# A ResNet block with Winograd rows: side taps read in unbroken runs, and a last unit with its outer positions last

## The chip, the cores and the metric

One core of one Trainium2 chip runs the whole kernel. The metric is device time in microseconds, from the median of three runs; the profile is one further execution, whose span is counted from its first to its last instruction.

## What is computed

Input x is 2 x 512 x 64 x 64 in bf16. The block normalises groups of 128 channels, applies silu, convolves 3 x 3 (512 to 512 channels), adds an embedding of the time step, normalises, applies silu, convolves again, and adds x:

```python
h = conv3(_silu(gn(x, g1, be1)), w1)
emb = _silu(t_emb) @ w_emb
h = h + emb.reshape(B, C, 1, 1)
h = conv3(_silu(gn(h, g2, be2)), w2)
return x + h
```

## The kernel before, in words

**Tiles.** Each image (2 of them) is cut into two halves of rows, each layer so into four chunks, eight in all (numbers c = 0 to 7; 4 to 7 are the second convolution). A chunk has four units, one for each block k of 128 output channels; 32 units (u = 0 to 31). A plane is eight rows of 65 elements a partition: 32 even columns, one column of zeros, 32 odd columns (`RW` = 65).

**The transform.** Along the image's height the convolution runs as Winograd with six positions s: 0 to 3 are the inner ones, 4 and 5 the outer ones. The outer ones, and in the first chunks some of the inner, stay direct along the width: `plain_mms` sums three taps kx, each a matmul of 512 columns (eight rows x 64), over four blocks ct of input channels, so twelve matmuls into one bank of PSUM. Tap 1 is the centre; taps 0 and 2, the side taps, need the even columns' neighbours among the odd ones and the other way round. The remaining inner positions are nested along the width too: `B_mms` and `A_mms` each do two matmuls of 256 columns a block. B reads and writes 256 columns in one run; A reads one run and writes eight runs of 32 with gaps of 32.

**A unit of the second layer.** In the order of its code: position 4, B of positions 0 and 2, position 5, B of 1 and 3, A of 0 and 2, A of 1 and 3. ACT evicts each pair of banks (`evac_b`, `evac_pair`, `evac_o`), DVE combines: the S additions out of the evicted B (`s_ops`), their addition to the evicted A, then s, d, three scalings (8, 2 and 4; in the last chunk ACT does the one by 2), two writes of 16 rows into `ys` (y), and the outer positions' addition (O). The last line stores `ys` onto the output with an accumulating DMA from POOL's queue; x itself has been copied to the output earlier, DRAM to DRAM, by two transfers of SP's queue a unit. The intermediate buffers exist once: `MB` (four slots of 512, M(0) to M(3)), `SD`, `BT`.

**The order.** All operations are first recorded with a cost and the regions that they read and write; a planner (`Plan.solve`) lays them out as a list schedule by the longest way to the end, and the program is emitted in that order. Matmuls keep the order in which they were recorded. For each chunk the planes of the next one are produced beside its units: load, silu on ACT, row combinations on DVE (`rows_a`, `rows_b`).

**Lines.** Most operations are recorded by helpers, so the profile names the helper's line: L380 all matmuls, L329 two-operand operations of DVE, L333 scalings of DVE, L352 everything of ACT, L365 all DMAs, L369 memsets. The tile `ar` is the one arena in SBUF in which all buffers lie.

Of the kernel before, what the change touches and what calls it, by code (L numbers as in the profile page):

```python
# [184 lines left out]
RW = 65  # L185
# [29 lines left out]
def kernel(  # L215
# [460 lines left out]
    def plain_mms(bank, c, k, ct, s):  # L676
        md = mode(c)
        vo = vplane(c, ct, s)
        lst = []
        for i, kx in enumerate((0, 2, 1)):  # L680
            if s < 4:
                w = um0(k, ct, kx, s)
            elif md != "1":
                w = ur0(k, ct, s - 4, kx)
            else:
                w = A(st_off(ucnt[0] % 2, ct) + (s - 4) * 384 + kx * 128, [[1, 128]], BF16)
            off, st = ((32, -32), (0, 33), (33, -32))[kx]
            rhs = A(vo + off, [[RW, 8], [st, 2], [1, 32]])
            lst.append((Ps(bank, 0, [[1, 512]]), w, rhs, ct == 0 and i == 0, ct == CT - 1 and i == 2))
        return lst  # L690

    def B_mms(bank, c, k, ct, s):
# [18 lines left out]
    def unit(c, k, opening=0):  # L711
        l, b, ch = chunks[c]
        md = mode(c)
        u = ucnt[0]
        nm = f"u{c}{k}"
        if opening != 1:
            ufirst[u] = len(pl.ops)
        last = u == 31
        ys = YS[u % 2]
        M = lambda i, n=1, st=512: A(MB + i * 512, [[st, n], [1, 512]]) if n > 1 else A(MB + i * 512, [[1, 512]])  # L720
        if md == "1":
            BT, SD = BT1, SD1
            OO = [UREG[2 * (u % 2) + 1] + 9728, UREG[2 * (u % 2)] + 9728]
        else:
            BT, SD = BT0, SD0
            OO = [O0[u % 3] + PL, O0[u % 3]]
        if l == 0 and ch == 0 and b not in SSUM:
            SSUM[b] = (Fc(48), Fc(2 * CT))
        acc = lambda i: None
        if l == 0:  # L730
            cs, cq = SSUM[b]
            acc = lambda i: F(cs + 12 * k + 6 * ch + i)
        fid = ACT.Identity if l == 0 else ACT.Copy

        def evac_o(s, bank):
            act(A(OO[s - 4], [[RW, 8], [33, 2], [1, 32]]), Ps(bank, 0, [[1, 512]]), fid,
                scale=(0.25, 1.0)[s - 4], acc=acc(s), name=nm + f"o{s}")

        def evac_m(s, bank, i):
            act(M(s), Ps(bank, 0, [[1, 512]]), fid, scale=KAP[s], acc=i, name=nm + f"m{s}")  # L740

        def evac_pair(s, bank):
            act(M(s, 2, 1024), Ps(bank, 0, [[512, 2], [1, 512]]), ACT.Copy, scale=KAP[s], name=nm + f"m{s}")

        def evac_b(s, bank):
            if md == "0":
                act(A(BT, [[1, 256]]), Ps(bank, 0, [[1, 256]]), ACT.Identity, scale=0.5 * KAP[0], acc=acc(0), name=nm + "b")
                act(A(BT + 256, [[1, 768]]), Ps(bank, 256, [[1, 768]]), ACT.Copy, scale=0.5 * KAP[0], name=nm + "b")
            else:
                act(A(BT + s * 512, [[1024, 2], [1, 512]]), Ps(bank, 0, [[512, 2], [1, 512]]), ACT.Copy,  # L750
                    scale=0.5 * KAP[s], name=nm + "b")

        def run(steps, major=False):
            todo = [(st, ct) for st in steps for ct in range(CT)]
            if major:
                todo = [(st, ct) for ct in range(CT) for st in steps]
            for (bank, s, fn), ct in todo:
                mm(fn(bank, c, k, ct, s), nm + f"{fn.__name__[0]}{s}")

        nf = {"N": 0, "0": 2, "1": 4}[md]  # L760

        def s_ops():
            g = lambda q: A(BT + q * 256, [[512, nf], [32, 8], [1, 32]])
            o, st = (SD + 512, -512) if md == "0" else (SD, 512)
            tt(A(o, [[st, nf], [64, 8], [1, 32]]), g(0), g(1), AD, nm + "S")
            tt(A(o + 32, [[st, nf], [64, 8], [1, 32]]), g(0), g(1), SB_, nm + "S")

        if opening == 1:
            return [lambda: evac_o(4, 2 * k), lambda: evac_o(5, 2 * k + 1)]
        if md == "N":  # L770
            p1, p2 = (0, 2) if u == 0 else (next_pair(), next_pair())
            if not opening:
                run([(6, 4, plain_mms)])
                evac_o(4, 6)
            if u == 0:
                run([(p1, 2, plain_mms), (p1 + 1, 0, plain_mms), (p2, 1, plain_mms), (p2 + 1, 3, plain_mms)], True)
            else:
                run([(p1, 2, plain_mms), (p1 + 1, 0, plain_mms)])
            evac_m(2, p1, acc(1))
            evac_m(0, p1 + 1, None)  # L780
            if not opening:
                run([(7, 5, plain_mms)])
                evac_o(5, 7)
            if u:
                run([(p2, 1, plain_mms), (p2 + 1, 3, plain_mms)])
            evac_m(1, p2, acc(3))
            evac_m(3, p2 + 1, acc(2))
        elif md == "0":
            p1, p2, p3 = next_pair(), next_pair(), next_pair()
            run([(6, 4, plain_mms)])  # L790
            evac_o(4, 6)
            run([(p1, 2, B_mms), (p1 + 1, 0, B_mms)])
            evac_b(0, p1)
            s_ops()
            run([(7, 5, plain_mms)])
            evac_o(5, 7)
            run([(p2, 2, A_mms), (p2 + 1, 0, A_mms)])
            evac_m(2, p2, acc(1))
            evac_m(0, p2 + 1, None)
            tt(M(0, 2, 1024), M(0, 2, 1024), A(SD, [[512, 2], [1, 512]]), AD, nm + "A")  # L800
            run([(p3, 1, plain_mms), (p3 + 1, 3, plain_mms)])
            evac_m(1, p3, acc(3))
            evac_m(3, p3 + 1, acc(2))
        else:
            p1, p2, p3, p4 = next_pair(), next_pair(), next_pair(), next_pair()
            run([(6, 4, plain_mms)])
            evac_o(4, 6)
            run([(p1, 0, B_mms), (p1 + 1, 2, B_mms)])
            evac_b(0, p1)
            run([(7, 5, plain_mms)])  # L810
            evac_o(5, 7)
            run([(p2, 1, B_mms), (p2 + 1, 3, B_mms)])
            evac_b(1, p2)
            s_ops()
            run([(p3, 0, A_mms), (p3 + 1, 2, A_mms)])
            evac_pair(0, p3)
            run([(p4, 1, A_mms), (p4 + 1, 3, A_mms)])
            evac_pair(1, p4)
            tt(M(0, 4), M(0, 4), A(SD, [[512, 4], [1, 512]]), AD, nm + "A")

        tw = lambda off, st: A(off, [[st, 2], [1, 512]])
        tt(tw(SD, 512), M(0, 2), M(2, 2), AD, nm + "s")
        tt(M(0, 2), M(2, 2), M(0, 2), SB_, nm + "d")
        se = CFG["s"][c]
        scal(se[0], M(2), M(1), 8.0, nm + "8")
        scal(se[1], M(3), M(1), 2.0, nm + "2")
        scal(se[2], A(SD + 1024, [[1, 512]]), A(SD + 512, [[1, 512]]), 4.0, nm + "4")
        yr = lambda r0: A(ys + r0 * RW, [[RW, 16], [33, 2], [1, 32]])
        tt(yr(0), A(MB, [[0, 2], [1, 512]]), A(MB + 1024, [[512, 2], [1, 512]]), AD, nm + "y")
        tt(yr(16), A(SD, [[0, 2], [1, 512]]), A(SD + 1024, [[-512, 2], [1, 512]]), AD, nm + "y")  # L830

        yo = A(ys, [[24 * RW, 2], [1, PL]])
        oo = A(OO[1], [[OO[0] - OO[1], 2], [1, PL]])
        if CFG["oacc"][l] and not last:
            dma(yo.ap, oo.ap, [oo, yo], [yo], P * 4 * PL, nm + "oa", sw=True, acc=True)
        else:
            tt(yo, yo, oo, AD, nm + "O")
        yv = A(ys, [[1, YF]])
        if l == 0:
            dma(h_scr[b, k, ch], yv.ap, [yv], [K("h", b, k, ch)], P * YF * 2, nm + "st")  # L840
            act(A8(JNK, YF), yv, ACT.Square, scale=float(HW) ** -0.5, acc=F(cq + ch * CT + k), name=nm + "sq")
            if ch == 1 and k == CT - 1:
                later.append(lambda: gn2(b))
        else:
            dma(out[b, k, ch], yv.ap, [yv], [K("o", b, k, ch, i) for i in range(2)], P * YF * 2, nm + "out", sw=True, acc=True)
        ucnt[0] += 1

    later = []
# [193 lines left out]
    for c in range(8):  # L1042
        l, b, ch = chunks[c]
        for k in range(CT):
# [16 lines left out]
                    memz("gpsimd", A(UREG[j] + 9728 + 32, [[RW, 8], [1, 1]]), "oz")  # L1061
            if l == 1:
                stream_w2(ucnt[0] % 2, k)
                for i in range(2):
                    r0, r1 = i * YF // 2, (i + 1) * YF // 2
                    dma(out[b, k, ch][:, r0:r1], x[b, k, ch][:, RW + r0:RW + r1], [], [K("o", b, k, ch, i)],
                        P * YF * 1.4, f"pre{c}{k}", after=ufirst[max(ucnt[0] - CFG["pre"], 0)])
# [83 lines left out]
```

## Time and profile before

| | |
|---|---|
| median of three runs | 500.62 us (500.51 to 501.32) |
| profiled execution, its span | 500.2 us; 0.4 us below the median of the runs |
| PE busy | 465.6 us (93%) |
| DVE busy | 434.1 us (87%) |
| ACT busy | 382.5 us (76%) |
| POOL busy | 37.8 us (8%) |
| matmuls of 512 columns, f16 | 1248, 295.5 us |
| matmuls of 256 columns, f16 | 1408, 164.8 us |

Matmuls are pipelined: a duration in the profile holds the way through the array too, so two durations overlap, and differences between durations say more than the durations. A row of a timeline gives the start, the length, the engine, the line and the operation, and in brackets the idle time ahead of it with what ended it. The clock column is the share of TensorE's clock that was granted; it is 1.00 in all stages from 136 us on, and 0.86 on average between 74.5 and 136. The profile's chain that ended last consists to 22% of time that nothing explains and stops at DMA issues of POOL, so I read the stages instead.

### The profile page before, as it was taken

How to read it: one execution, taken by the hardware profiler on the slowest of the kernel's cores; microseconds unless marked ns; L12 is line 12 of the kernel's file. 1: busy time of each engine (PE TensorE's matmuls, PEld its weight loads, DVE VectorE, ACT ScalarE, POOL GpSimd, SP SyncE). 2: the span in 40 equal slices, each digit the busy share in tenths (PEclk: the TensorE clock that was granted, in tenths of full speed). 3: DMA queues.
4: the chain of work that ended last, by engine and by line, in shares of the span. 5: the costliest groups of instructions: out<-in, count | busy, mean ns of one | idle time of the engine just before them, and what ended most of it. 6: DMA issues, size and time to landing. Idle time of an engine off the chain costs nothing. (4 is left out here: it accounts for less than half of the span.)

```text
span 500.2 us, 8097 instructions
## 1 busy us (share of the span) xinstructions
PE 465.6 (93%) x2853; PEld 276.9 (55%) x2853; DVE 434.1 (87%) x856; ACT 382.5 (76%) x614; POOL 37.8 (8%) x66
## 2 busy tenths in 40 slices
PE   6999999686699999999999999999999999999980
PEld 5744344253345455555554567666666666666660
DVE  1699999997769999997999999997999999985553
ACT  4886899999699978679987887777765888565440
POOL 3100000000100000110000001103011110011000
PEclk9999999988599999999999999999999999999996
DMA  8754463465723336576576887677676768557232
GB/s 330 281 171 113 156 177 111 167 201 164 237 85 120 119 108 180 171 213 237 201 244 219 294 285 206 167 192 135 194 194 187 201 171 247 108 106 150 44 43 43
DMA packets 41064, 87.17 MB, mean 174 GB/s; under 512 B 6464, under 2 KB 16448, under 8 KB 41024
## 3 DMA queue, kind: packets, MB, share of 16 engines
q1 hardware_dynamic: 35808, 77.07, 46.5%
q0 software_dynamic: 4928, 9.59, 12.9%
q8 instruction: 22, 0.36, 0.3%
q14 instruction: 18, 0.15, 0.1%
q10 hardware_dynamic: 288, 0.01, 0.0%
HBM read 62.25 MB, written 31.85 MB: 188 GB/s over the span
## 5 line engine op out<-in xcount | busy, mean ns | idle before, releaser
L380 PE MATMUL psum<-ar 128*128 128x256 f16 (+2 forms) x2737 | 450.4, 326 | 9.0 <-DVE ar L329 4.3
L329 DVE TENSOR_TENSOR ar<-ar 128x1040 f16<-128x1040 f16 (+6 forms) x682 | 404.9, 651 | 39.5 <-ACT ar L352 35.1
L380 PEld LDWEIGHTS <-ar 128*128 128x128 f16 (+1 forms) x2729 | 264.3, 98 | 192.2 <-issue 16.1
L352 ACT ACTIVATE ar<-ar 128x384 bf16<-128x384 bf16 (+6 forms) x206 | 169.6, 854 | 45.6 <-DVE ar L329 41.6
L352 ACT ACTIVATE ar<-psum 128x512 f16<-128x512 f32 (+2 forms) x221 | 153.8, 718 | 51.1 <-PE psum L380 42.3
L352 ACT ACTIVATE ar<-ar,fs 128x2112 f16<-128x2112 bf16 (+1 forms) x32 | 68.6, 2148 | 6.9 <-DMA ar<-h_scr 5.1
L365 POOL DMA_DIRECT2D out_dram<-ar x16 | 19.3, 1207 | 129.1 <-DVE ar L329 129.0
L333 DVE TENSOR_SCALAR ar<-ar 128x512 f16<-128x512 f16 (+2 forms) x72 | 26.0, 382 | 2.0 <-ACT ar L352 2.0
L352 ACT ACTIVATION_READ_ACCUMULATOR ar<-psum 128x1 f32 x96 | 19.6, 204 | 0.0
L451 POOL TENSOR_TENSOR fs<-fs 128x1 f32<-128x1 f32 (+1 forms) x7 | 7.0, 996 | 138.2 <-DVE fs L449 138.2
L380 PE MATMUL psum<-ar,ones_bf 128*128 128x260 bf16 x64 | 9.5, 307 | 4.7 <-DMA ar<-in_x_dram 4.7
L369 POOL MEMSET ar<- 128x65 f16 (+4 forms) x27 | 4.1, 195 | 114.5 <-DVE ar L329 41.9
L380 PE MATMUL psum<-fs,ones_neg 128*128 128x1 f32 (+3 forms) x36 | 5.2, 258 | 7.0 <-DVE fs L982 6.9
L352 ACT ACTIVATION_READ_ACCUMULATOR ar<-ar 128x1 f32 x56 | 11.0, 197 | 0.0
L380 PEld LDWEIGHTS <-ones_bf 128*128 128x128 bf16 x64 | 6.6, 108 | 6.4 <-issue 3.4
L380 PEld LDWEIGHTS psum<-fs,ones_neg 128*128 128x128 f32 x36 | 5.0, 206 | 8.0 <-DVE fs L982 7.2
L365 POOL DMA_DIRECT2D ar<-ar x4 | 3.7, 930 | 72.3 <-DVE ar L329 56.4
L913 DVE SCALAR_TENSOR_TENSOR ar<-psum,ident 128x128 bf16<-128x128 f32 x4 | 1.2, 290 | 5.6 <-PE psum L380 5.6
L993 DVE BATCH_NORM_STATS2 fs<-ar 128x6 f32<-128x512 bf16 x8 | 5.3, 681 | 0.0
L442 DVE COPY fs<-psum 128x2 f32<-128x2 f32 (+1 forms) x7 | 1.1, 161 | 4.5 <-PE psum L380 4.5
L415 DVE CAST fs<-gparm 128x16 f32<-128x16 bf16 x1 | 0.2, 190 | 2.8 <-DMA gparm<-in_params_dram 2.8
L411 ACT ACT_TABLE_LOAD x1 | 1.3, 1283 | 1.7 <-PEq L1135 1.7
(49 smaller groups left out, 23.4 us busy)
## 6 DMA issues: line engine op xcount, KB each, us to landing
ar<-in_w_dram SPq DMA_DIRECT2D x32, 384.0 KB, 3.9
ar<-in_x_dram SPq DMA_DIRECT2D x16, 552.5 KB, 4.0
h_scr<-ar SPq DMA_DIRECT2D x16, 520.0 KB, 3.2
ar<-h_scr SPq DMA_DIRECT2D x16, 520.0 KB, 4.0
out_dram<-in_x_dram SPq DMA_DIRECT2D x32, 260.0 KB, 4.2
out_dram<-ar POOLq DMA_DIRECT2D x16, 520.0 KB, 6.4
u_scr<-ar SPq DMA_DIRECT2D x16, 384.0 KB, 3.2
ar<-u_scr SPq DMA_DIRECT2D x4, 1536.0 KB, 7.6
```

What stands on the lines that cost most here:

```text
L329: pl.op("DVE", 0.075 + 0.000521 * out.n, lambda: nc.vector.tensor_tensor(out=out.ap, in0=a.ap, in1=b.ap, op=op), regs(a, b), regs(out), name)
L333: pl.op("DVE", cost or 0.075 + 0.00026 * out.n, lambda: nc.vector.tensor_scalar(out=out.ap, in0=a.ap, scalar1=s, scalar2=None, op0=ALU.mul ...
L352: lambda: nc.scalar.activation(out=out.ap, in_=a.ap, func=func, scale=sc, **kw), regs(*rr), regs(*ww), name)
L365: lambda: eng.dma_start(out=out, in_=in_, **kw), regs(*r), regs(*w), name, lat=3.2 if sw else None, after=after, sw=sw)
L369: pl.op("POOL" if eng == "gpsimd" else "DVE", 0.08 + 0.0005 * out.n, lambda: e.memset(out.ap, v), (), regs(out), name)
L380: nc.tensor.matmul(out.ap, lhsT=lhsT.ap, rhs=rhs.ap, start=st, stop=sp, skip_group_check=True)
L411: nc.scalar.activation(out=fs[:, WARM:WARM + 1], in_=fs[:, WARM + 1:WARM + 2], func=ACT.Silu)
L415: nc.vector.tensor_copy(out=fs[:, GB:GB + 4 * CT], in_=gparm[:])
L442: pl.op("DVE", 0.16, lambda: V.tensor_copy(out=F(tot, 2 * n).ap, in_=ps.ap), regs(ps), regs(F(tot, 2 * n)), name)
L451: pl.op("POOL", 0.85, lambda: nc.gpsimd.tensor_tensor(out=F(rs, n).ap, in0=N.ap, in1=F(NEGH, n).ap, op=ALU.pow), regs(N), regs(F(rs, n)), ...
L913: pl.op("DVE", 0.3, lambda: nc.vector.scalar_tensor_tensor(out=j2.ap, in0=g.ap, scalar=1.0 / HW, in1=ident[:], op0=ALU.mult, op1=ALU.mult, ...
L993: pl.op("DVE", 0.61, lambda e=e, q=q: nc.vector.bn_stats(out=q.ap, in_=e.ap), regs(e), regs(q), nm)
```

## The change

Two places, and what follows from the second.

In `plain_mms` the side taps' read and write change places: the read takes 64 elements of a row as they lie, beginning at the row's first column (tap 0) or its second (tap 2), and the write puts the first 32 of each row to the odd and the second 32 to the even columns. The centre tap stays.

The last unit (u = 31) gets a function of its own. Its matmuls run in the order B, B, A, A, position 4, position 5. x is loaded into SBUF and not copied to the output beforehand; DVE adds it to d and s before the scalings, and writes y in pieces of eight rows in bf16. The output goes out in three plain stores from SP's queue: rows 8 to 23, then 24 to 31, then 0 to 7. Position 5 is not evicted by ACT; DVE adds it straight out of PSUM.

```diff
-            off, st = ((32, -32), (0, 33), (33, -32))[kx]
-            rhs = A(vo + off, [[RW, 8], [st, 2], [1, 32]])
-            lst.append((Ps(bank, 0, [[1, 512]]), w, rhs, ct == 0 and i == 0, ct == CT - 1 and i == 2))
+            if kx == 1:
+                rhs, o = A(vo, [[RW, 8], [33, 2], [1, 32]]), Ps(bank, 0, [[1, 512]])
+            else:
+                rhs, o = A(vo + kx // 2, [[RW, 8], [1, 64]]), Ps(bank, 32, [[64, 8], [-32, 2], [1, 32]])
+            lst.append((o, w, rhs, ct == 0 and i == 0, ct == CT - 1 and i == 2))
...
+        if last:
+            return last_unit(c, k, run, evac_b, evac_pair, evac_o, s_ops, M, SD, OO)
...
+    def last_unit(c, k, run, evac_b, evac_pair, evac_o, s_ops, M, SD, OO):
+        l, b, ch = chunks[c]
+        nm = "ul"
+        ys, yb, dx = YS[1], VB[0], VB[0] + 2112
+        xt = AB[acnt[0] % 2]
+        d = A(xt, [[1, YF]], BF16)
+        dma(d.ap, x[b, k, ch][:, RW:RW + YF], [], [d], P * YF * 2, nm + "x")
+        memz("gpsimd", A(yb + 32, [[RW, 32], [1, 1]], BF16), nm)
+        p1, p2, p3, p4 = next_pair(), next_pair(), next_pair(), next_pair()
+        run([(p1, 0, B_mms), (p1 + 1, 2, B_mms)])
+        evac_b(0, p1)
+        run([(p2, 1, B_mms), (p2 + 1, 3, B_mms)])
+        evac_b(1, p2)
+        s_ops()
+        run([(p3, 0, A_mms), (p3 + 1, 2, A_mms)])
+        evac_pair(0, p3)
+        run([(p4, 1, A_mms), (p4 + 1, 3, A_mms)])
+        evac_pair(1, p4)
+        run([(6, 4, plain_mms)])
+        evac_o(4, 6)
+        run([(7, 5, plain_mms)])
...
+        tt(M(0, 2, 1024), M(0, 2, 1024), tw(SD, 1024), AD, nm + "A")
+        tt(one(SD), M(0), M(2), AD, nm + "s")
+        tt(one(SD + 1024), M(2), M(0), SB_, nm + "d")
+        tt(tw(dx, 512), A(SD + 1024, [[0, 2], [1, 512]]), xr(0), AD, nm + "x")
+        tt(tw(dx + 1024, 512), A(SD, [[0, 2], [1, 512]]), xr(16), AD, nm + "x")
+        tt(M(1, 2, 1024), M(1, 2, 1024), tw(SD + 512, 1024), AD, nm + "A")
+        tt(M(0), M(3), M(1), SB_, nm + "d")
+        tt(M(2), M(1), M(3), AD, nm + "s")
+        ts(M(1), M(0), 2.0, nm + "2")
+        tt(row(yb, 8, BF16), one(dx + 512), M(1), AD, nm + "y")
+        ts(M(3), M(2), 4.0, nm + "4")
+        tt(row(yb, 16, BF16), one(dx + 1024), M(3), AD, nm + "y")
...
+        st(8, 16)
+        tt(row(ys, 24), one(dx + 1536), M(2), AD, nm + "y")
+        ts(M(1), M(0), 8.0, nm + "8")
+        tt(row(ys, 0), one(dx), M(1), AD, nm + "y")
+        tt(row(yb, 24, BF16), row(ys, 24), row(OO[0], 0), AD, nm + "O")
+        st(24, 8)
+        o5 = Ps(7, 0, [[1, 512]])
+        pl.op("DVE", 0.68, lambda: nc.vector.tensor_tensor(
+            out=row(yb, 0, BF16).ap, in0=row(ys, 0).ap, in1=o5.ap, op=AD), regs(row(ys, 0), o5), regs(row(yb, 0)), nm + "O")
+        st(0, 8)
...
-                for i in range(2):
+                for i in range(2 if ucnt[0] < 31 else 0):
```

Only the end of each engine's order moves; ahead of it the instructions stand as before, but for the form of the side taps' writes. On DVE the end of the program before, from unit 30's s and d (1024 x2) on, where 16x2x32 is a write of y, 2x520 the addition O, 32x32 an S addition, and 2048 the addition to the evicted A:

```order
636 L329 TENSOR_TENSOR ar<-ar 128x1024 x2
637 L333 TENSOR_SCALAR ar<-ar 128x512 x2
638 L329 TENSOR_TENSOR ar<-ar 128x16x2x32 x2
639 L329 TENSOR_TENSOR ar<-ar 128x2x520
640 L329 TENSOR_TENSOR ar<-ar 128x32x32 x2
641 L329 TENSOR_TENSOR ar<-ar 128x2048
642 L329 TENSOR_TENSOR ar<-ar 128x1024 x2
643 L333 TENSOR_SCALAR ar<-ar 128x512 x2
644 L329 TENSOR_TENSOR ar<-ar 128x16x2x32 x2
645 L329 TENSOR_TENSOR ar<-ar 128x2x520
```

The same place of the change, from unit 30's writes of y on (L898 is the addition out of PSUM):

```order
638 L329 TENSOR_TENSOR ar<-ar 128x16x2x32
639 L329 TENSOR_TENSOR ar<-ar 128x32x32
640 L329 TENSOR_TENSOR ar<-ar 128x16x2x32
641 L329 TENSOR_TENSOR ar<-ar 128x32x32
642 L329 TENSOR_TENSOR ar<-ar 128x2x520
643 L329 TENSOR_TENSOR ar<-ar 128x2x512
644 L329 TENSOR_TENSOR ar<-ar 128x512
645 L329 TENSOR_TENSOR ar<-ar 128x2x512
...
651 L329 TENSOR_TENSOR ar<-ar 128x8x2x32 x2
652 L333 TENSOR_SCALAR ar<-ar 128x512
653 L329 TENSOR_TENSOR ar<-ar 128x8x2x32 x3
654 L898 TENSOR_TENSOR ar<-ar,psum 128x8x2x32
```

The S additions of unit 31 have moved between unit 30's writes of y, and unit 31's own chain has become twelve rows of smaller operations. On ACT, the end as a difference (2x512 is the eviction of a pair of banks, 8x2x32 that of an outer position, `ar<-ar` the scaling by 2):

```order
-L352 ACTIVATE ar<-psum 128x2x512 x3
-L352 ACTIVATE ar<-psum 128x8x2x32
-L352 ACTIVATE ar<-ar 128x512
-L352 ACTIVATE ar<-psum 128x2x512
-L352 ACTIVATE ar<-psum 128x8x2x32
-L352 ACTIVATE ar<-psum 128x2x512 x3
-L352 ACTIVATE ar<-ar 128x512
...
+L352 ACTIVATE ar<-psum 128x2x512 x5
+L352 ACTIVATE ar<-ar 128x512
+L352 ACTIVATE ar<-psum 128x2x512 x2
+L352 ACTIVATE ar<-psum 128x8x2x32
```

Unit 30's scaling now stands behind both B evictions of unit 31, the A evictions follow it, and one outer position's eviction is gone.

More of the change, by code (lines that the diff above doesn't have):

```diff
@@ L845, in unit @@
             dma(out[b, k, ch], yv.ap, [yv], [K("o", b, k, ch, i) for i in range(2)], P * YF * 2, nm + "out", sw=True, acc=True)
+        ucnt[0] += 1
+    def last_unit(c, k, run, evac_b, evac_pair, evac_o, s_ops, M, SD, OO):
[19 more added lines that the diff above has]
+        run([(7, 5, plain_mms)])
+        tw = lambda off, st: A(off, [[st, 2], [1, 512]])
+        one = lambda off: A(off, [[1, 512]])
+        xr = lambda r0: A(xt + r0 * RW, [[RW, 16], [33, 2], [1, 32]], BF16)
+        row = lambda base, r0, dt=None: A(base + r0 * RW, [[RW, 8], [33, 2], [1, 32]], dt)
+        tt(M(0, 2, 1024), M(0, 2, 1024), tw(SD, 1024), AD, nm + "A")
[10 more added lines that the diff above has]
+        tt(row(yb, 16, BF16), one(dx + 1024), M(3), AD, nm + "y")
+        st = lambda r0, n: dma(out[b, k, ch][:, r0 * RW:(r0 + n) * RW], A(yb + r0 * RW, [[1, n * RW]], BF16).ap,
+                               [A(yb + r0 * RW, [[1, n * RW]], BF16)], [K("o", b, k, ch, r0)], P * n * RW * 2, nm + "out")
+        st(8, 16)
[8 more added lines that the diff above has]
+        st(0, 8)
```

## The prediction

> **What bounds the kernel now.** I read the busy time by stage first, with the stage borders laid where an engine changes its part. Columns: stretch in us, its length, then busy time and instruction count of PE, PEld, DVE, ACT and POOL, the granted clock, the DMA share and GB/s.
>
> ```profile
> 37.00:74.50 37.50, 37.50 (x168) 15.58 (x168) 36.28 (x78) 32.31 (x77) 0.00 (x0) 1.00 0.50 150
> 74.50:136.00 61.50, 46.75 (x213) 22.09 (x213) 55.34 (x122) 54.05 (x123) 1.26 (x1) 0.86 0.55 177
> 136.00:145.00 9.00, 9.00 (x48) 4.54 (x47) 3.90 (x7) 9.00 (x13) 0.00 (x0) 1.00 0.26 81
> 145.00:174.00 29.00, 28.75 (x162) 15.45 (x160) 28.66 (x58) 28.39 (x46) 0.00 (x0) 1.00 0.34 119
> 174.00:218.00 44.00, 44.00 (x248) 23.86 (x248) 42.81 (x98) 31.40 (x64) 4.49 (x6) 1.00 0.51 152
> 218.00:245.00 27.00, 27.00 (x155) 14.73 (x154) 23.65 (x49) 26.46 (x45) 1.34 (x4) 1.00 0.63 206
> 245.00:343.00 98.00, 98.00 (x628) 60.68 (x627) 96.98 (x177) 75.86 (x108) 6.41 (x13) 1.00 0.74 223
> 343.00:360.00 17.00, 17.00 (x127) 12.13 (x126) 13.65 (x23) 14.34 (x16) 1.51 (x3) 1.00 0.89 227
> 360.00:394.00 34.00, 33.86 (x234) 22.52 (x232) 33.86 (x55) 23.69 (x27) 2.70 (x4) 1.00 0.64 175
> 394.00:474.00 80.00, 79.92 (x578) 56.18 (x578) 66.81 (x106) 52.83 (x65) 9.94 (x10) 1.00 0.65 147
> 474.00:486.30 12.30, 12.29 (x88) 8.31 (x86) 6.21 (x10) 5.83 (x7) 1.20 (x1) 1.00 0.31 43
> 486.30:500.30 14.00, 0.00 (x0) 0.00 (x0) 4.92 (x8) 1.65 (x2) 1.20 (x1) 0.67 0.26 38
> ```
>
> Two things stand in it. From 136 to 486 PE never rests, so it looks like the only bound. But another engine is as full in most stages: ACT (9.00 of 9.00, then 26.46 of 27) or DVE (28.66 of 29, 96.98 of 98, 33.86 of 34). Only 394 to 474, 343 to 360 and, by 1.2 us, 174 to 218 leave both of them room. And the last 14 us have no matmul at all. How close DVE and ACT run to PE shows in PE's own timeline at two chunk borders, where it waits a moment for them:
>
> ```profile
> 173.92 0.62 PE L380 MATMUL psum<-ar 128*128 128x512 f16 x2 [0.25 <-DVE ar L329]
> 394.08 0.38 PE L380 MATMUL psum<-ar 128*128 128x256 f16 x2 [0.22 <-ACT ar L352]
> ```
>
> So up to 394 PE and the pair DVE/ACT arrive together; only after it is PE alone the bound. Then the end, by the timeline of ACT, DVE and POOL (start, length, what, idle before):
>
> ```profile
> 473.98 1.02 ACT L352 ACTIVATE ar<-psum 128x1024 f16<-128x1024 f32 x1 [0.78 <-PE psum L380]
> 475.04 2.68 DVE L329 TENSOR_TENSOR ar<-ar 128x2048 f16<-128x2048 f16 x3 [2.26 <-ACT ar L352]
> 477.63 0.49 DVE L333 TENSOR_SCALAR ar<-ar 128x512 f16<-128x512 f16 x2
> 478.04 2.02 DVE L329 TENSOR_TENSOR ar<-ar 128x1024 f16<-128x1024 f16 x3
> 483.89 1.29 DVE L329 TENSOR_TENSOR ar<-ar 128x1024 f16<-128x1024 f16 x2 [3.83 <-ACT ar L352]
> 486.38 1.02 ACT L352 ACTIVATE ar<-psum 128x1024 f16<-128x1024 f32 x1 [0.78 <-PE psum L380]
> 490.44 2.02 DVE L329 TENSOR_TENSOR ar<-ar 128x1024 f16<-128x1024 f16 x3
> 492.76 1.20 POOL L365 DMA_DIRECT2D out_dram<-ar  x1 [11.20 <-DVE ar L329]
> out_dram<-ar POOLq DMA_DIRECT2D x1, 520.0 KB, 5.8
> ```
>
> The first ACT row marks the end of unit 30's matmuls (473.9), the second the end of unit 31's (486.3). Behind the latter come 1.1 us of eviction, 5.0 us of DVE (487.44 to 492.46), an accumulating store issued by POOL at 492.76 that lands after 5.8 us (492.8 + 5.8 = 498.6), and 1.6 us from there to the span's end at 500.2.
>
> **Part 1, the side taps.** 832 of the 1248 matmuls of 512 columns keep their count and columns; their read becomes eight runs of 64 instead of sixteen of 32 that jump to and fro, their write sixteen runs of 32 that jump. What each costs, by duration (min/median/max in the second and in the last two rows, which are one contiguous-write and one strided-write piece of a unit):
>
> ```profile
> L380 PE MATMUL psum<-ar 128*128 128x512 f16 x866 | 203.9, 387 | 0.2 <-DVE ar L329 0.2
> L380 PE MATMUL psum<-ar x11: 383/387/392, 441.0 to 443.2; 128*128 128x512 f16 x11
> L380 PE MATMUL psum<-ar,s_sb 128*2 128x512 bf16 x9 | 2.4, 378 | 0.0
> L380 PE MATMUL psum<-ar x15: 272/273/273, 443.7 to 445.2; 128*128 128x256 f16 x15
> L380 PE MATMUL psum<-ar x15: 272/273/273, 445.5 to 447.1; 128*128 128x256 f16 x15
> ```
>
> The minimum, 383, is the centre tap; with a mean of 387 the two side taps take (3 x 387 - 383) / 2 = 389. A matmul of 512 that reads and writes one unbroken run takes 378 (the embedding's). So a side tap can win 6 ns (like the centre), at most 11 (like the unbroken one), or nothing, if the jumping write costs what the jumping read did. I take 8: the new read breaks at the same eight places as the centre's (one skipped column a row), in half as many runs, and the write side has shown no price. That is the last pair of rows: the pieces B write 256 columns in one run, the pieces A in eight runs of 32 with gaps, and both take 273.
>
> Here a rule speaks against the change. The Trainium skill, "PSUM — Partial Sum Buffer", section "Specifications (TRN2)", says that any access pattern that isn't contiguous slows matmuls significantly, PSUM's lines being 8 bytes. The trace doesn't bear that out: 273 against 273. By the rule a side tap would get dearer and not cheaper, which is the last rival below.
>
> What of 8 ns a tap arrives at the end? From 136 to 474 there are 866 such matmuls, 577 side taps, 4.6 us on PE. But where DVE or ACT is full a faster PE only waits longer at the next border. What comes through is the stages with room:
>
> ```profile
> L380 PE MATMUL psum<-ar 128*128 128x512 f16 x146 | 35.1, 387 | 0.0
> L380 PE MATMUL psum<-ar 128*128 128x512 f16 x30 | 7.3, 387 | 0.0
> ```
>
> These are 394 to 474 and 343 to 360: (146 + 30) x 2/3 = 117 side taps, 0.9 us. Of 37 to 74.5 and 174 to 218, where DVE idles 1.2 us each, I add 0.3. Before 136 the rest goes into waits that DVE ends (PE has 14.75 of 61.5 us idle there). Together 1.2 us earlier at the end of unit 30; from below 0, from above 577 x 11 = 6.3.
>
> **Part 2, the last unit.** PE's work is the same in another order: B, B, A, A, then the two outer positions. So the evictions of the A pieces come while PE still has the 24 matmuls of 512 ahead. Kept on the times above, without part 1: PE ends unit 31 at 486.3 again. DVE decides. From 475.04 it does, without a pause:
>
> - unit 30's 2048, 1024, 1024 and two scalings as now, up to 478.04;
> - y, S, y, S, O instead of y, y, O: 2.02 + 1.29 = 3.31, up to 481.35. This S, now 2.5 us earlier than it was, finds its B evictions done: ACT does them at 475.7 and 477.5 (PE has 1.75 us a piece), and unit 30's own scaling on ACT stands behind them, done by 479.2, before the y that reads it;
> - the new chain: four of 1024 elements, four of 512, three scalings of 512, five writes of 512 to y rows. The A evictions wait until y has read their slots and end at about 481.0, just under cover: if DVE were 0.3 us earlier it would wait for ACT.
>
> ```profile
> L329 DVE TENSOR_TENSOR ar<-ar 128x1024 f16<-128x1024 f16 x10 | 6.6, 689 | 4.0 <-ACT ar L352 3.8
> L329 DVE TENSOR_TENSOR ar<-ar 128x512 f16<-128x512 f16 x72 | 28.1, 427 | 0.2 <-ACT ar L352 0.2
> L333 DVE TENSOR_SCALAR ar<-ar 128x512 f16<-128x512 f16 x40 | 10.1, 287 | 0.0
> L1016 DVE COPY ar<-psum 2x512 f32<-2x512 f32 x1 | 0.7, 680 | 0.3 <-PE psum L380 0.3
> ```
>
> 4 x 0.689 + 9 x 0.427 + 3 x 0.287 = 7.46. Neighbours that don't depend on each other overlap (two of 0.689 take 1.29, not 1.38): 0.085 each for 13 of 16, so 6.4, up to 487.75. By then PE has ended, 1.4 us before, so the last addition doesn't wait for it. That one reads PSUM; no row shows it. Between 0.43 (the SBUF addition) and 0.68 (the copy out of PSUM of as many f32) I take 0.65, nearest to the row that reads PSUM: 488.4.
>
> The last store is a plain one of 130 KB on SP's queue, whose other entries are then long done. It too is bounded by rows:
>
> ```profile
> ar<-in_w_dram SPq DMA_DIRECT2D x32, 96.0 KB, 2.4
> u_scr<-ar SPq DMA_DIRECT2D x16, 384.0 KB, 3.2
> ```
>
> Between 2.4 and 3.2, and below that, since the queue is otherwise empty, perhaps 2.0; I take 2.4, with 0.1 for SP to wake: 490.9. The other two pieces are issued 0.6 us and more earlier. With the same 1.6 us to the span's end: 492.5, against 500.2. **Part 2 brings 7.7 us.** From both sides: without any overlap on DVE and with 3.2 to land 494.4; with 0.43 and 2.0, 491.9.
>
> At nothing I cost: the load of x (520 KB on SP, into a buffer that chunk 7's production has left, some 40 us before it is read; the six weight loads behind it wait for slots anyway), the memset on POOL (waits for chunk 6's matmuls, 6 us before the next store there is due), and two transfers of 260 KB less. If the x load came late it would hold those weights, and then PE.
>
> **Sum.** 500.2 - 7.7 - 1.2 = 491.3 of span. The median of the runs shown (500.62) stands 0.4 above the profiled span, so 491.7.
>
> **The rivals.**
> - The side taps stay at 389, the write's jumps costing what the read's did. For it: the same permutation, only moved. Against: 273 = 273. Part 2 alone: 492.5 + 0.4 = 492.9.
> - PE's gain arrives whole, because DVE and ACT gain from earlier evictions. For it: in many places DVE and ACT wait for PE's evictions, not only for themselves. Against: DVE 96.98 of 98 has nothing left to gain. 500.2 - 7.7 - 4.6 + 0.4 = 488.3.
> - The new end is longer: operations of 512 don't overlap, the small store lands late, DVE waits for the A evictions. 494.4 + 0.4 - 0.5 for some of part 1 = about 494.3.
> - Slower: the jumping write stalls the matmul. Place: 577 side taps between 136 and 474 with PE the bound throughout. It decides from 7.7 / 577 = 13 ns above 389, thus 402. At 2 ns a jump, 30 ns a tap, PE alone needs 577 x 30 = 17.3 us more: 500.2 - 7.7 + 17.3 + 0.4 = 510. For it: the rule above, and that no matmul of the trace writes backwards. Against: the gaps of the A pieces cost nothing.
>
> **How the numbers follow.** The forecast has 0.60, side taps unchanged 0.17, the whole gain 0.10, a longer end 0.07, slower 0.05, and 0.01 for a gain that just cancels. The range that should hold 8 in 10: the forecast's ends are 491.1 and 494.4 for the tail, less up to 3 us for part 1, so 488 to 495; it takes in the unchanged taps, the longer end and most of the whole gain. A change of 0.2% (1.0 us) is about what this measurement can tell from none: faster 0.94, same 0.01, slower 0.05.
>
> **What would show it.** Part 1: in the group of 512 columns a mean of about 382 instead of 387; more PE idle at the borders near 174 and 394, DVE as full as before, and 394 to 474 shorter by about 0.8 us. Part 2: DVE busy without a gap from the end of unit 30 to an addition out of PSUM that ends some 2 us behind the last matmul; SP's last store landing in 2 to 3 us; 6 us instead of 14 from the last matmul to the end. It is wrong if that mean is over 389, if PE waits within the last unit, or if DVE there waits for ACT by more than 0.3 us.

## The result

The changed kernel takes 490.15 us (median of four runs, 490.06 to 490.70) against 500.97 us (500.51 to 501.62) before: 0.9785 of the time, 95% interval 0.9771 to 0.9799. That is 10.8 us less; 8.9 were forecast (500.62 to 491.7). The time lies inside the range and the sign is right, but the two parts did not bring what the sum gave them, as the following shows. The profiled execution has a span of 488.9 us; its own time is 490.7, so 1.8 us lie around the span. The same 1.8 holds for the profiled executions of the four runs of the first series below. If it holds for the profile of before as well, that execution took 502.0, longer than all timed runs of before, and did not lie below their median as I took it.

The busy time by stage after the change (columns as in the prediction):

```profile
168.00:212.00 44.00, 43.08 (x245) 23.85 (x244) 42.84 (x98) 34.18 (x69) 4.49 (x6) 1.00 0.54 162
242.00:339.00 97.00, 95.77 (x620) 60.41 (x619) 94.72 (x172) 75.32 (x108) 6.41 (x13) 1.00 0.72 224
357.00:392.00 35.00, 34.55 (x241) 23.34 (x239) 34.83 (x57) 23.33 (x25) 2.70 (x4) 1.00 0.62 175
392.00:471.60 79.60, 79.41 (x578) 56.46 (x578) 66.91 (x106) 52.85 (x64) 10.18 (x11) 1.00 0.66 148
471.60:483.94 12.34, 12.34 (x89) 8.37 (x86) 10.97 (x22) 6.12 (x7) 1.20 (x1) 1.00 0.25 34
483.94:488.94 5.00, 0.00 (x0) 0.00 (x0) 1.95 (x6) 0.00 (x0) 0.00 (x0) 0.85 0.43 129
```

PE, which hardly rested before, now does: 0.9 us in the first of these stages, 1.2 in the second, 0.45 in the third. The stretch behind the last matmul has gone from 14 us to 5.0.

PE's waits from 136 us to the end of unit 30, first of the kernel before, then of the changed one (total us, how often, longest):

```profile
PE psum L380 <- DVE ar L329: 0.2, 1, 0.2
PE psum L380 <- ACT ar L352: 0.2, 1, 0.2
```

```profile
PE psum L380 <- DVE ar L329: 1.3, 2, 0.9
PE psum L380 <- DVE fs L442: 1.2, 1, 1.2
PE psum L380 <- ACT ar L352: 0.3, 1, 0.3
```

0.4 us have become 2.8. The matmuls of 512 columns in that stretch, and one piece of a unit (min/median/max):

```profile
L380 PE MATMUL psum<-ar 128*128 128x512 f16 x862 | 200.2, 386 | 2.2 <-DVE fs L442 1.2 <-DVE ar L329 0.9
L380 PE MATMUL psum<-ar x10: 386/386/388, 439.3 to 441.3; 128*128 128x512 f16 x10
```

All three taps now take 386 to 387, where the centre took 383 and the sides 389. From start to start in the trace the three taps together take 667.5 ns instead of 677. That is 9.5 for two side taps, 4.7 each.

And the end, by DVE's timeline:

```profile
472.76 2.68 DVE L329 TENSOR_TENSOR ar<-ar 128x2048 f16<-128x2048 f16 x3 [2.26 <-ACT ar L352]
475.36 0.49 DVE L333 TENSOR_SCALAR ar<-ar 128x512 f16<-128x512 f16 x2
475.76 7.23 DVE L329 TENSOR_TENSOR ar<-ar 128x1024 f16<-128x1024 f16 x13
482.91 0.49 DVE L333 TENSOR_SCALAR ar<-ar 128x512 f16<-128x512 f16 x2
483.32 0.76 DVE L329 TENSOR_TENSOR ar<-ar 128x512 bf16<-128x512 f16 x2
483.99 0.29 DVE L333 TENSOR_SCALAR ar<-ar 128x512 f16<-128x512 f16 x1
484.19 1.10 DVE L329 TENSOR_TENSOR ar<-ar 128x512 bf16<-128x512 f16 x3
485.20 0.68 DVE L898 TENSOR_TENSOR ar<-ar,psum 128x512 bf16<-128x512 f16 x1
```

The three stores on SP's queue, and the landing of the two small ones (count, size, median us from issue):

```profile
484.68 1.56 SPq L365 DMA_DIRECT2D out_dram<-ar  x3
```

```profile
out_dram<-ar SPq DMA_DIRECT2D x2, 130.0 KB, 1.8
```

DVE works without a gap from 472.76 to 485.89, 1.95 us behind the last matmul (483.94). The last store is issued right behind it, lands 1.8 us later, and 1.2 us after that the span ends at 488.94.

### The profile page after: what moved, and what is told of

Its sections match the earlier page's. It is cut to its first block, busy times and chain, and to the rows that moved or that the text cites. A ratio compares the mean times of both kernels' runs of the same rounds, so it can differ in the third digit from the quotient of the medians.

```text
span 488.9 us, 8107 instructions
## 1 busy us (share of the span) xinstructions
PE 460.8 (94%) x2853; PEld 279.1 (57%) x2853; DVE 435.8 (89%) x865; ACT 379.8 (78%) x612; POOL 37.4 (8%) x66
## 3 DMA queue, kind: packets, MB, share of 16 engines
q1 hardware_dynamic: 36096, 77.60, 47.7%
## 5 line engine op out<-in xcount | busy, mean ns | idle before, releaser
L380 PE MATMUL psum<-ar 128*128 128x256 f16 (+2 forms) x2737 | 445.5, 325 | 11.7 <-DVE ar L329 5.7
L380 PEld LDWEIGHTS <-ar 128*128 128x128 f16 (+1 forms) x2729 | 266.5, 99 | 187.6 <-issue 17.3
L365 POOL DMA_DIRECT2D out_dram<-ar x15 | 18.1, 1206 | 108.9 <-DVE ar L329 108.9
L369 POOL MEMSET ar<- 128x65 f16 (+5 forms) x28 | 4.4, 197 | 123.6 <-DVE ar L329 47.2
L453 DVE TENSOR_TENSOR fs<-fs 128x1 f32<-128x1 f32 (+1 forms) x7 | 1.1, 155 | 1.9 <-POOL fs L451 1.9
```

The lines of the kernel that those rows point to most:

```text
L365: lambda: eng.dma_start(out=out, in_=in_, **kw), regs(*r), regs(*w), name, lat=3.2 if sw else None, after=after, sw=sw)
L369: pl.op("POOL" if eng == "gpsimd" else "DVE", 0.08 + 0.0005 * out.n, lambda: e.memset(out.ap, v), (), regs(out), name)
L380: nc.tensor.matmul(out.ap, lhsT=lhsT.ap, rhs=rhs.ap, start=st, stop=sp, skip_group_check=True)
L453: small(lambda: V.tensor_mul(out=S.ap, in0=F(rs, n).ap, in1=F(g, n).ap), [F(rs, n)], [S], name)
```

## The experiments

Each is the changed kernel with one thing different, unless said otherwise. One program differs from run to run by 0.5 to 3 us, so besides the medians I use stages: the time between the first matmuls of two units (found by counting a trace's matmuls in their order), and from the first matmul of unit 31 to the end of the span. In the expectations and here, units 12, 23, 41, 42 and 61 are named by chunk and block (unit 61 is block 1 of chunk 6, u = 25); units 30 and 31 are u = 30 and 31, the last two. The tail alone is 26.5 us in the profile of before and 17.5 in that of the change.

**Each part alone.** Without the call of `last_unit` and with the copies of x restored, only the side taps are new:

```diff
-        if last:
-            return last_unit(c, k, run, evac_b, evac_pair, evac_o, s_ops, M, SD, OO)
...
-                for i in range(2 if ucnt[0] < 31 else 0):
+                for i in range(2):
```

> Side taps in the new form, last unit as before. Theory (a side tap is 6 ns cheaper; DVE and ACT swallow most of it; what arrives is 0.9 us before 100 us and 1.4 us because PE, coming back earlier from its wait near 129 us, finds its full clock one step of 3.4 us earlier): 2.3 us under before, about 498.5; the half-clock stretch at 122 us lasts 10.2 us and not 13.7. Rival, the whole gain arrives (832 x 6 ns = 5.0 us): about 496. Rival, the gain of the change is all in the last unit: within 0.5 us of before.

Measured: 499.28 us (498.43 to 499.43) against 501.05, ratio 0.9962, interval 0.9947 to 0.9976. So the taps alone bring 1.8 us in the median, between 1.2 and 2.7. PE's waits from 136 to 474 us are 2.0 us instead of 0.4. The half-clock stretch lasted 13.7 us and not 10.2, so that part of the theory missed.

With the old lines of `plain_mms` and the new last unit:

> Old side taps, new last unit. Theory: end of unit 30's matmuls as before (473.9 in the trace), from there to the end of the span 17.3 us instead of 26.3: 9 us under before, about 492.0. As forecast: 7.7 us under before. Rival, the two parts share a gain: less than 7. The half-clock stretch at 122 us lasts 13.7 us as before.

Measured: 491.37 us (491.16 to 492.17), ratio 0.9806 (0.9789 to 0.9822), 9.7 us less; from unit 31's first matmul to the end of the span 17.7 us. The new unit is worth 8.8 us by the stage, more than forecast. The half-clock stretch was 10.2 us, with the old taps, and not 13.7.

**The taps in half of the chunks.** The old form is kept where the chunk is not in the list; for late it reads as follows, for early with `c < 4`.

```diff
+            if kx != 1 and not (c >= 4):
+                off, st = ((32, -32), (0, 33), (33, -32))[kx]
+                rhs, o = A(vo + off, [[RW, 8], [st, 2], [1, 32]]), Ps(bank, 0, [[1, 512]])
```

> New last unit; new side taps in chunks 4 to 7 alone (256 side taps, 1.5 us on PE). Theory: the second layer's stages with room let 0.4 us through, so 0 to 0.5 us under unit_only. Rival, whole gain: 1.5 us under unit_only. Half-clock stretch as before, 13.7 us.

> New last unit; new side taps in chunks 0 to 3 alone (576 side taps, 3.4 us on PE). Theory: about 2 us under unit_only, nearly all of the changed kernel's gain, 1.4 us of it from the shorter half-clock stretch at 122 us (10.2 us). Rival, whole gain: 3.4 us under unit_only. Rival, the clock step came by chance of the run and not by the taps: 0.5 to 1 us under unit_only, with 13.7 us of half clock.

Measured: late 491.16 (490.97 to 491.50), early 491.91 (490.27 to 492.98), against 491.37 for none of them. Late is 0.2 us less, too little for the medians to tell from none, but not the 1.5 of the whole gain. Early should have brought 2 us and brought nothing visible, in a spread of 2.7 us. The half-clock stretches lasted 13.7 and 10.2 us, as expected. From unit 61's first matmul to the last unit's, the stage in which PE alone is the bound, the traces say it plainly: 74.4 us before, in unit_only and in taps_early; 74.0 in the changed kernel, in taps_only and in taps_late. That is 0.4 us, wherever chunks 6 and 7 have the new taps.

**The half-clock stretch.** My explanation after the result was that PE, returning 0.9 us sooner from its wait near 129 us, found its full clock one step earlier. To see whether equal programs agree, I ran the change again, as a yardstick:

> The changed kernel once more, as the yardstick for the three beside it: 490.0 to 490.7. If the stretches of half clock before 140 us differ from run to run for the same program, the traces of equal programs differ by 1 to 2 us there and by less than 0.3 us from the last matmul to the end (5.0 us).

Measured: 490.33 us (489.72 to 492.56; two of the five at 492.55, three under 490.4). Here are the stages 129 to 132.4 and 132.4 to 136 of the changed kernel, then of the same program again (the column behind POOL is the granted clock):

```profile
129.00:132.40 3.40, 2.99 (x8) 1.05 (x8) 3.28 (x10) 0.77 (x2) 0.93 (x1) 0.50 0.80 243
132.40:136.00 3.60, 3.60 (x26) 2.42 (x25) 1.61 (x6) 2.29 (x4) 0.33 (x1) 1.00 0.63 208
```

```profile
129.00:132.40 3.40, 1.62 (x4) 0.54 (x4) 3.29 (x9) 1.74 (x5) 0.00 (x0) 0.50 0.88 290
132.40:136.00 3.60, 3.60 (x10) 1.30 (x9) 1.86 (x7) 0.39 (x1) 1.26 (x1) 0.50 0.70 220
```

The same program, and 26 matmuls against 10 in the second stage. Unit 12 begins at 140.6 in the one and at 143.1 in the other. Some 1.1 of these 2.5 us arise earlier, where the second execution alone ran at half clock, from 95.3 to 98.7 us. The theory of the clock step falls: the place of the half-clock stretches differs from run to run, whatever the taps.

How much they make shows from the first matmul of chunk 1 to that of unit 12. It takes 46.7 to 46.8 us in the four traces with stretches of 3.4 and 13.7 us, two with the old taps there (before, taps_late) and two with the new (taps_only, forms); 45.3 to 45.4 in four with 3.4 and 10.2 (the changed kernel, outer_first, one_store, tail2); 47.7 in again and taps_early, which have one more of 3.4. The spans of before and after differ by 11.3 us, 9.0 of it in the tail, and the other 2.3 stand there already at unit 12 (142.8 and 140.6); 1.4 of them are this stage, so by these traces the clock's and not the taps'. From the last matmul to the end both take 5.0 us, as expected.

**What a side tap's price consists of.** Four forms of the side taps, one to a chunk:

```diff
+                if c in (2, 5):
+                    rhs = A(vo + kx // 2, [[1, 512]])
+                if c in (3, 5):
+                    o = Ps(bank, 0, [[1, 512]])
+                if c == 6:
+                    rhs = A(vo + off, [[RW, 8], [st, 2], [1, 32]])
```

> The changed kernel with other side taps in four chunks, whose output is therefore not the convolution there: chunk 2 reads 512 columns in one run and writes with the jump; chunk 3 reads rows of 64 and writes straight; chunk 5 reads one run and writes straight; chunk 6 has the old to-and-fro read and writes with the jump; 4 and 7 stay new. Durations of a side tap if the read sets the cost: chunk 2 378 ns, 3 386, 5 378, 6 390. If the jumping write costs: chunk 2 386, 3 378, 5 378, 6 over 390. If each costs half: chunk 2 and 3 382.

One piece of twelve each (min/median/max), in the order of chunks 2, 3, 5, 6:

```profile
L380 PE MATMUL psum<-ar x12: 377/388/392, 199.2 to 201.7; 128*128 128x512 f16 x12
L380 PE MATMUL psum<-ar x12: 382/383/386, 255.7 to 258.2; 128*128 128x512 f16 x12
L380 PE MATMUL psum<-ar x12: 379/380/386, 359.8 to 362.2; 128*128 128x512 f16 x12
L380 PE MATMUL psum<-ar x12: 383/388/389, 409.7 to 412.2; 128*128 128x512 f16 x12
```

None of the three answers fits whole. Both unbroken: 380, as the embedding's 378. Row reads with a straight write: 382, so the jumping write costs some 4 of the 386. One long read with the jumping write: one side tap at 377, the other at 391 and the centre behind it at 388, so no gain at all (from start to start 668 ns for the three). The old read with the jumping write: as the old form, 677, so there the jump adds nothing. So the jump of the write is not free behind a row read, and the costs of read and write don't add up; why the tap that begins at an odd element is dear only there, the run doesn't say.

**The order in the last unit.** Positions 4 and 5 ahead of B and A:

```diff
+        run([(6, 4, plain_mms)])
+        evac_o(4, 6)
+        run([(7, 5, plain_mms)])
         run([(p1, 0, B_mms), (p1 + 1, 2, B_mms)])
...
-        run([(6, 4, plain_mms)])
-        evac_o(4, 6)
-        run([(7, 5, plain_mms)])
```

> The changed kernel's last unit with positions 4 and 5 ahead of B and A, all else as changed. Theory (the late positions cover DVE's chain; without them it starts after the last A eviction): the end comes about 8.6 us behind the last matmul instead of 5.0, so some 3.5 us over the changed kernel, near 493.7. Rival (the order is worth nothing, the gain is the plain store and x added beforehand): within 0.5 us of the changed kernel.

Measured: 494.38 us (494.12 to 497.07), 4.2 over the changed kernel, and 9.4 us from the last matmul to the end. The stretch behind the last matmul (482.95 here):

```profile
482.95:492.36 9.41, 0.00 (x0) 0.00 (x0) 6.29 (x17) 1.02 (x1) 0.00 (x0) 0.71 0.16 57
```

6.3 us of DVE stand where 1.95 did; its last operation:

```profile
488.62 0.68 DVE L898 TENSOR_TENSOR ar<-ar,psum 128x512 bf16<-128x512 f16 x1
```

The rival falls. By the stage the tail is 21.9 us. So of its 9.0 us, 4.4 come from the order. The remaining 4.6 lie at the store: from DVE's last operation to the end of the span it is 7.8 us in the profile of before (492.46 to 500.24) and 3.1 here (489.30 to 492.36), as in the change. No run changes the kind of the store alone, but by these stretches the plain store in pieces brings them; x is added early so that it can be plain.

**One store instead of three.**

```diff
-        st(8, 16)
...
-        st(24, 8)
...
-        st(0, 8)
+        st(0, 32)
```

> The changed kernel with one plain store of 520 KB behind the last addition instead of three pieces. Theory: the two early pieces hide three quarters of the bytes; the one store lands 1.0 to 1.3 us later, near 491.3. Rival (landing is a fixed time whatever the size): within 0.3 us of the changed kernel. From the last addition to the end of the span: 4.1 to 4.4 us against 3.05.

The store's landing:

```profile
out_dram<-ar SPq DMA_DIRECT2D x1, 520.0 KB, 2.6
```

Measured: 490.47 us (490.25 to 490.97), 0.3 over the changed kernel. 3.6 us from the last addition to the end instead of 3.05. 520 KB land in 2.6 us, 130 KB in 1.8. The pieces are worth 0.6 us, half of what I expected.

**Scalings of chunk 3 on ACT.** Two of three scalings per unit go from DVE to ACT:

```diff
-    's': ((A_, A_, A_), (D_, D_, D_), (D_, A_, A_), (D_, D_, D_), (A_, A_, A_), (A_, A_, D_), (A_, A_, A_), (D_, A_, D_)),
+    's': ((A_, A_, A_), (D_, D_, D_), (D_, A_, A_), (A_, D_, A_), (A_, A_, A_), (A_, A_, D_), (A_, A_, A_), (D_, A_, D_)),
```

> The changed kernel with two of the three scalings of chunk 3's units on ACT instead of DVE (about 2 us less on DVE between 227 and 284; the planner lays the order out anew). Theory (DVE's load there turns PE's gain into the 1.2 us wait of unit 41's position 5): that wait goes below 0.3 us, and unit 42 starts 0.8 to 1.2 us sooner after unit 23. Rival (the wait is the latency of the second normalisation's chain, whatever DVE's load): wait unchanged within 0.2 us.

Its waits of PE from 136 to 474:

```profile
PE psum L380 <- DVE ar L329: 0.8, 1, 0.8
PE psum L380 <- DVE fs L442: 0.5, 1, 0.5
```

Measured: 488.85 us (488.67 to 490.31), ratio 0.9774 (0.9759 to 0.9790); the interval overlaps that of the change. From unit 23 to unit 42 96.57 us instead of 97.28: 0.7 less, just the 0.7 by which the wait on line 442 shrank (1.2 to 0.5), though it didn't go below 0.3. DVE's timeline ahead of that copy, in the changed kernel and then here:

```profile
294.88 7.27 DVE L329 TENSOR_TENSOR ar<-ar 128x1040 f16<-128x1040 f16 x11
302.06 0.16 DVE L442 COPY fs<-psum 128x8 f32<-128x8 f32 x1
```

```profile
294.74 6.66 DVE L329 TENSOR_TENSOR ar<-ar 128x1024 f16<-128x1024 f16 x10
301.31 0.16 DVE L442 COPY fs<-psum 128x8 f32<-128x8 f32 x1
```

PE waits for a copy that stands behind a run of DVE without a gap, and here one addition fewer stands ahead of it. That a smaller load of DVE does it isn't shown. The planner laid out a new order from 23 us on, and DVE has 95.6 us of work in the 96.57 from unit 23 to 42, against 93.5 in 97.28; work of later units moved ahead (from unit 61 to the last one DVE has 55.6 us instead of 61.6). The wait near 386 to 392 us (0.7 us in the trace of the change, 0.2 in that of again) is gone too, and unit 42 to unit 61 takes 86.3 us instead of 87.2 and 86.7.

**Versions that go further.** The last chain shortened: x of the outer rows enters PSUM by matmuls with the identity, two scalings on ACT.

```diff
+                lst.insert(1, (Ps(bank, 0, [[1, 512]]), id4 if s == 4 else cid,
+                               A(xt + (24 if s == 4 else 0) * RW, [[RW, 8], [33, 2], [1, 32]], BF16), False, False))
...
-        tt(tw(dx, 512), A(SD + 1024, [[0, 2], [1, 512]]), xr(0), AD, nm + "x")
+        tt(one(dx + 512), one(SD + 1024), row(xt, 8, BF16), AD, nm + "x")
...
+        scal("ACT", M(3), M(2), 4.0, nm + "4")
+        scal("ACT", one(dx), M(0), 8.0, nm + "8")
```

> The changed kernel with a shorter last chain on DVE: x of the outer rows enters PSUM by two matmuls with the identity (and four times it) instead of DVE's additions, two of the last scalings go to ACT. Theory (DVE bounds the end, 1.3 us behind PE): DVE 0.9 us shorter, PE 0.4 us longer, the end of the last addition from 1.95 us behind the last matmul to about 0.7; 0.8 us less from the end of unit 30 to the end of the span (17.5 to 16.7). Rival (ACT's scalings come late and DVE waits for them): within 0.3 us of the yardstick.

```profile
475.72 6.68 DVE L329 TENSOR_TENSOR ar<-ar 128x1024 f16<-128x1024 f16 x13
482.32 0.28 DVE L333 TENSOR_SCALAR ar<-ar 128x512 f16<-128x512 f16 x1
482.52 1.77 DVE L329 TENSOR_TENSOR ar<-ar 128x512 f16<-128x512 f16 x5
484.38 0.69 DVE L909 TENSOR_TENSOR ar<-ar,psum 128x512 bf16<-128x512 f16 x1
```

The stage does what it should: the last addition ends 0.7 us behind the last matmul (484.34), and unit 31 to the end takes 16.7 instead of 17.5. The median doesn't show it: 490.86 (489.86 to 491.78) beside 490.33.

> The shorter last chain and chunk 3's two scalings on ACT: 0.7 us less than tail2 in the stage from unit 23 to unit 42, with the wait of unit 41's position 5 at about 0.5 us; about 488.7.

Measured: 488.18 us (488.09 to 489.71), ratio 0.9758 (0.9744 to 0.9773), the fastest of all, beyond the interval of the yardstick in the same series (0.9786 to 0.9831). By the stages it gains 0.8 at the end, 0.7 between units 23 and 42, and 0.4 to 1.0 between units 42 and 61, as act_c3 did there.

> As tail2_c3, and the third scaling of chunk 5's units on ACT too (0.8 to 1.1 us less on DVE between 335 and 384). Theory (DVE's load in chunk 5 makes PE's wait of 0.8 to 1.0 us around 386 to 393): that wait halves and the end comes 0.3 to 0.6 us sooner than in tail2_c3. Rival (that wait is set by ACT or by the load of h): no difference over 0.2 us.

Measured: 489.03 us (488.31 to 489.83), not faster. The expected wait around 386 to 393 us is in neither trace: PE doesn't wait there in tail2_c3 nor here, and unit 42 to unit 61 takes 86.3 us in both. So the run can't decide between theory and rival. What differs is the wait on line 442, 1.0 instead of 0.5: in the new order the copy comes 0.6 us later.

## Why the prediction was right, and where not

- **That PE and the pair DVE/ACT arrive together up to 394** was right, and it is why the whole gain didn't come. The taps save (677 - 667.5) x 866 / 3 = 2.7 us of PE from 136 to the end of unit 30. PE's waits there grew from 0.4 to 2.8, by 2.4. The longest, 1.2 us, is for a copy that stands behind 7.3 us of DVE without a gap.
- **The size of a side tap** was too large: 8 ns put, 4.7 measured from start to start; the mean duration went to 386 and not to about 382, since the centre tap rose to 386. The step that failed is "the write side has shown no price". The A pieces, whose gaps cost nothing, are no evidence for a write that jumps back and forth: forms shows 4 ns for it behind row reads.
- **What comes through of it**: 1.2 us put. Between unit 12 and unit 31 the two traces even agree within 0.1 us (330.9); six traces of programs with all the new taps and no other change there give 329.9 to 331.0, 330.4 in the mean, two with the old ones 330.7 and 330.9. Where equal programs agree to 0.1 us, the traces show three pieces. Chunk 0, from its first matmul to that of chunk 1, gains 0.65 us: 73.7 in the three traces with old taps there, 73.05 to 73.07 in the eight with new ones and the same order. From unit 23 to 42 0.4 us are lost: 96.8 to 96.9 with the old taps, 97.2 to 97.3 with the new, because PE comes 0.8 us sooner to unit 41 but waits 1.2 there. From unit 61 on 0.4 are gained, all that a tap of 4.7 ns can bring there, where 0.9 were put for this stage and that from 343 to 360. That makes 0.65. By the medians it is 1.8 for taps_only and 1.2 for the change over unit_only; the rest, where the clock scatters or equal programs differ by 0.6 us (units 42 to 61), stays open. That the 1.2 put lies so near is luck: the tap was put too dear, and chunk 0 was put at next to nothing.
- **The gain of the last unit** was put too small: 18.6 us put from the end of unit 30's matmuls to the end of the span, 17.3 measured. DVE's chain was right (14.5 put, 14.3 measured; the addition out of PSUM 0.65 put, 0.68 measured). What failed is the store: 2.4 us put for the landing, with 2.0 as the lowest; 1.8 measured; and 1.2 us from there to the end, not the 1.6 that the accumulating store of before had. Also right: DVE ends about 2 us behind PE; the eviction of the A pieces waits on DVE's y and comes just in time.
- **The profile's place among the runs** was read wrongly. If 1.8 us lie around the span of before too, that execution took about 1 us longer than the median, and the 0.4 added to the span is too little for a time of its own. The two cancel, because the sum takes a difference from the median (500.62 - 8.9). The range's ends are not of one kind either: 491.1 already holds part 1 and the 0.4, 494.4 is the tail's span alone.
- **The rule of the Trainium skill** that access which isn't contiguous slows matmuls (the Trainium skill, "PSUM — Partial Sum Buffer", "Specifications (TRN2)") has something in it for this write: 386 with the jump, 382 without, both behind row reads. But it is 4 ns of 386, far from the 13 more that would have made the change slower.

## What to carry to other kernels

When one engine shows 100% busy, look at how full the others are stage by stage before crediting a saving on it: here a saving of 2.7 us on PE turned into 2.4 us of waits, and another order on DVE, with one addition fewer ahead of a copy that PE waits for, gave 0.7 of it back. At the end of a program, order the last work so that the longest chain on the other engines runs beside matmuls that need little after them, and end in a plain store of a small piece: here 4.4 us came from the order and, by the stretches, 4.6 from the store. With a difference of about 1 us, compare stages of traces, not spans, since the clock's steps fall differently from execution to execution.

## What was unexpected of the hardware

- A matmul that reads one unbroken run and writes with the jump is not cheaper than one that reads eight runs: 377, 391 and 388 for the three taps, against 386 to 387.
- The centre tap, which was not changed, follows its neighbours' read: 383 behind the old read with either write, 386 behind row reads with either write, and 386 and 388 behind one long read with the straight and the jumping write.
- The half-clock stretch after PE's idle time near 120 us ended at 132.4 and at 136.2 in two executions of one program; with one more stretch of 3.4 us near 95 us in the second, unit 12 began 2.5 us later.
